# First blocks' loads, masks and three moved steps in an attention, expert and mixing kernel

## The chip, the cores and the metric

The kernel runs on one core of a Trainium2 chip. The metric is the device time of one execution, in microseconds (us). A core has five engines that run side by side, each with its own queue of instructions in a fixed order: TensorE (PE; its weight loads are listed as PEld), VectorE (DVE), ScalarE (ACT), GpSimd (POOL) and SyncE (SP), which here only issues DMAs. ScalarE and GpSimd issue DMAs too. They wait for one another by semaphores.

## The reference

Three parts follow one another. The attention keeps a window of `n_local` = 96 keys and the first `n_global` = 8 keys, adds a bias that falls with the distance, and takes the softmax. The result goes token by token through one of eight experts (a gate decides whether a token takes its own best expert or that of the token before it). A last part mixes over tokens and channels, with a sine and a cosine of a projected angle.

```python
scores = scale * np.matmul(q, k.transpose(0, 1, 3, 2))       # 2 x 8 heads, 768 x 768, head size 64
keep = is_global | is_local
bias = -slopes[:, None, None] * dist[None, :, :]
scores = np.where(keep, scores + bias[None], -1e9)
a = softmax(scores)                                          # rows sum to one
x = a @ v                                                    # -> (2, 768, 512)
...
h = np.maximum(x[b, s] @ w1[e], 0.0)
out[b, s] = p[e] * (h @ w2[e])                               # e: expert of the token
...
theta = x @ w_theta
y = w_tok_r @ (x * cos(theta)) + w_tok_i @ (x * sin(theta))
u = x + y
result = u + np.maximum(u @ w_ch, 0.0)
```

## The kernel before, in words

**Attention.** The 768 tokens of each of two batches are cut into 6 tiles of 128, so there are 12 blocks. `BLOCKS` takes them tile by tile, both batches of a tile in turn; blocks 0 and 1 are the first tiles. A block has four units of two heads. A step `s` is two units, so there are 24 steps, and steps 0 to 3 belong to the first two blocks. In a step TensorE makes the scores of its two units (`qk`, line 558), VectorE adds the bias and takes the extreme of each row (`soft`, line 580), ScalarE takes the exponential (line 590), and TensorE transposes the probabilities of the step before (line 613) and multiplies those of two steps before with the values (line 637). A first tile needs only its own 128 keys; any other needs 256: the 96 before it, 32 of the beginning (for the global keys) and its own 128. The tile `kall` holds 160 key columns for each tile of tokens, and a block reads 256 of them in a row, so the second tile reads the last 96 columns of the first tile's keys.

**Start.** SP issues the window sizes `nn` (line 132), then queries and keys (`load_qk`, lines 466 and 467) and values (`load_v`) of blocks 0, 1 and 2. Block 0's queries and keys come in two halves, so there are four loads for it, in runs of 512 bytes. VectorE casts `nn` (line 508), runs four mask operations (`mask0`, lines 511 to 514) and scales the mask for each head (`biases`, line 525): `biases(0, 0)` and `biases(0, 1)` ahead of the first scores, `biases(0, 2)` and `biases(0, 3)` in step 0. GpSimd makes the constants and then the mask and biases of all other tiles. TensorE starts with `NWARM` = 10 products on zeros (`warm`, line 861) and has one or two of them after the scores of steps 0 to 4 (`WARM`).

**Order by hand.** Every operation of the attention has a short name (`lt10` is the transposed logits of block 10, `pl4` the place of pair 4's tokens in their experts' lists, `px` and `pc` the transpose and copy of the first expert's rows, `lc` the copy of the logits to `lT`, `tk` the token counts). Within the steps they are run by the loop at the end of the attention; what is left after step 23 is listed in `TAIL`. The logits, the token positions and the routing share one bank of TensorE's output memory, the tile `small`.

**Weight jobs.** The weights of the last part (26 pieces, 512 columns each, stored as 64-bit numbers) are converted by `job`: six steps, the absolute value on ScalarE with a shift on VectorE (lines 401 and 402), two integer operations (404, 406), a product (408), a copy on ScalarE with the load of a later piece (411), a difference (414). `job_tick` runs one step. `JATT` lists the attention steps that have one at their end; `TAIL` has three (`jt`); in the expert rounds `tick` adds `JRATE[r]`, divided by 4.5 for rounds 1 to 3 and by 6 otherwise, and runs a step for each whole number reached. `tick` is called from unit 5 on up to unit 55 (a round is eight units), six times per unit, in rounds 1 to 3 not in units 2 and 3, and in rounds 4 to 7 twelve times in every second unit. In the last part `job_upto` (its first call comes with block 1) finishes the job at hand and all that the next product needs.

**Expert rounds.** Rounds 4 to 6 take their weights as they are for the first product (line 1474) and split in two for the second (ScalarE line 1455, VectorE line 1456, TensorE line 1547).

**Last part.** For each block TensorE makes the angle (`th`, line 1783), VectorE and ScalarE reduce it and take sine and cosine (lines 1793 to 1810; line 1797 is the first that reads the product and frees its bank), and TensorE mixes (line 1859).

Of the kernel before, what the change touches and what calls it, by code (L numbers as in the profile page):

```python
# [9 lines left out]
F32 = mybir.dt.float32  # L10
F32R = mybir.dt.float32r
BF16 = mybir.dt.bfloat16
I32 = mybir.dt.int32
AF = mybir.ActivationFunctionType
ALU = mybir.AluOpType
# [35 lines left out]

BLOCKS = [b * NT + t for t in range(NT) for b in range(B)]
TWO_PI = 6.283185307179586
NWARM = 10

WARM = {0: 1, 1: 2, 2: 1, 3: 1, 4: 1}

TAIL = """
ev10 ro4 tk3 tr46 tr47 sc4 cp46 oh4 ho4 cp47 pv44 pv45 yt10 po4 lg10 ri10 lc10 pl4 px pc lt10 ys10 ld10 pv46 pv47 ev11
ri11 mk4 ha0 hb0 hr0 jt yt11 lg11 lc11 jt ha1 hb1 hr1 lt11 ld11 ya0 yb0 sl4 ch5 tk4 ha2 hb2 hr2 ro5 sc5 ys11 ya1 yb1 oh5  # L60
ho5 ha3 hb3 hr3 po5 pl5 ya2 yb2 mk5 rk ha4 hb4 hr4 sl5 tk5 ya3 yb3 ha5 hb5 hr5 en ya4 yb4 ha6 hb6 hr6 ya5 yb5 ha7 hb7
hr7 ya6 yb6 ya7 yb7 ye jt
# [5 lines left out]
CPV0 = (1, 3)  # L68


JATT = (4, 5, 6, 8, 9, 10, 12, 13, 14, 16, 17, 19, 20, 21, 22)
JRATE = (2.0, 1.2, 1.3, 2.9, 2.6, 2.3, 0.4)
T1, T2, T3 = 2, 2, 2
JBUFS = 3
HS = 8
# [25 lines left out]
def kernel(  # L101
# [13 lines left out]
    V, A, G, PE, SP = nc.vector, nc.scalar, nc.gpsimd, nc.tensor, nc.sync  # L115

    const = ctx.enter_context(tc.tile_pool(name="const", bufs=1))
    res = ctx.enter_context(tc.tile_pool(name="res", bufs=1))
# [3 lines left out]
    def ct(shape, dt, name):  # L122
        return const.tile(shape, dt, name=name, tag=name)
# [5 lines left out]


    nn = ct([128, 4], I32, "nn")
    SP.dma_start(nn, n_win.bitcast(I32).partition_broadcast(128))
    wg = ct([128, 4, 32], F32, "wg")


# [216 lines left out]
    wch = [res.tile([128, 4, DM], F32R, tag=f"wch{i}", name=f"wch{i}") for i in range(2)]  # L352
# [93 lines left out]
    with ExitStack() as actx:  # L446
# [4 lines left out]
        pX = actx.enter_context(tc.tile_pool(name="pX", bufs=1, space=PSUM))  # L451
        pM = actx.enter_context(tc.tile_pool(name="pM", bufs=1, space=PSUM))

        qs, vals = {}, {}

        kall = res.tile([128, B, 4, NT * 160], F32, tag="wtokr1", name="kall")

        def load_qk(i):
            n = BLOCKS[i]
            b, t = divmod(n, NT)  # L460
            q = qs[n] = ab.tile([128, 4, 128], F32, tag="q", name="q", bufs=3)
            src = pack[b, t, :, 0:1152].rearrange("p (j c) -> p j c", j=4)
            o = 0 if t else 32

            for j in (slice(0, 2), slice(2, 4)) if n == 0 else (slice(0, 4),):
                SP.dma_start(q[:, j], src[:, j, 0:128])
                SP.dma_start(kall[:, b, j, t * 160 + o : t * 160 + 160], src[:, j, 128 + o : 288])

        def load_v(i):
            n = BLOCKS[i]  # L470
# [8 lines left out]
        wm = ap.tile([128, 512], BF16, tag="wm", name="wm", bufs=1)  # L479
        V.memset(wm, 0.0)  # L480
        G.memset(wg, 0.0)
        for load, i in ((load_qk, 0), (load_qk, 1), (load_v, 0), (load_qk, 2), (load_v, 1), (load_v, 2)):
            load(i)
        for hh in range(2):
            SP.dma_start(
# [4 lines left out]
        wl, wgl = nf[:, 0:1], nf[:, 2:3]  # L490
# [6 lines left out]
        rel = ab.tile([128, 384], F32, tag="rel", name="rel", bufs=1)  # L497
        drop = ab.tile([128, 384], F32, tag="drop", name="drop", bufs=1)
# [9 lines left out]
        V.tensor_copy(nf, nn)  # L508

        def mask0():  # L510
            V.tensor_scalar(rel[:, 0:128], rel[:, 0:128], wl, None, op0=ALU.min)
            V.tensor_scalar(drop[:, 0:128], temp["iota"][:, 0:128], wgl, DROP, op0=ALU.is_ge, op1=ALU.mult)
            V.scalar_tensor_tensor(drop[:, 0:128], rel[:, 0:128], wl, drop[:, 0:128], op0=ALU.is_ge, op1=ALU.mult)
            V.tensor_tensor(drop[:, 0:128], rel[:, 0:128], drop[:, 0:128], op=ALU.add)

        def mask1():
            G.tensor_scalar(drop[:, 128:384], rel[:, 128:384], wl, DROP, op0=ALU.is_ge, op1=ALU.mult)
# [4 lines left out]
        def biases(t, j):  # L522
            bias, c = (bias1, slice(128, 384)) if t else (bias0, slice(0, 128))
            for h in (2 * j, 2 * j + 1):
                (G if t else V).tensor_scalar(bias[:, h], drop[:, c], -8.0 * 2.0 ** -(h + 1), None, op0=ALU.mult)
# [22 lines left out]
        def qk(s):  # L548
            n = units[2 * s][0]
            b, t = divmod(n, NT)  # L550
            W = 256 if t else 128
            for i in range(2):

                sp = [pS.tile([128, 256], F32, tag=f"s{hh}", name=f"s{hh}") for hh in range(2)]
                j = units[2 * s + i][1]
                for hh in range(2):
                    half = slice(64 * hh, 64 * hh + 64)
                    PE.matmul(  # L558
                        sp[hh][:, 0:W],
                        lhsT=qs[n][half, j],  # L560
                        rhs=kall[half, b, j, t * 160 + 160 - W : t * 160 + 160],
                        start=True,
                        stop=True,
                    )
                ust[2 * s + i] = {"s": [x[:, 0:W] for x in sp]}
# [349 lines left out]
        def run(names):  # L915
            for k in names.split():
                ops[k]()
# [5 lines left out]

        warm(NWARM)
        biases(0, 0)
        biases(0, 1)
        mask1()
        for j in range(4):
            biases(1, j)
# [1 line left out]
        for s in range(NS):  # L931
# [4 lines left out]
            qk(s)  # L936
            warm(WARM.get(s, 0))
            run(later.pop((s, 0), ""))
            run(f"sa{u} sb{u}")
            run(later.pop((s, 1), ""))  # L940
            if s:
                run(f"tr{u - 2} tr{u - 1} cp{u - 2}")
# [7 lines left out]
            if s >= 2:  # L950
                run(f"pv{u - 4} pv{u - 3}")
                if s % 2:
                    i, t = s // 2 - 1, (s // 2 - 1) // B
# [20 lines left out]
            if s in (1, 2):  # L974
                job_load()
            if s in JATT:
                job_tick()
# [391 lines left out]
    with ExitStack() as mctx:  # L1369
# [260 lines left out]
        for u in range(64):  # L1630
            r, f = divmod(u, 8)
# [77 lines left out]
            i = f - (1 if r else GP)  # L1709
# [12 lines left out]
            i = f - (2 if r else XF)  # L1722
# [4 lines left out]
    with ExitStack() as hctx:  # L1727
# [260 lines left out]
        for k in range(1, NB):  # L1988
            b, t = divmod(k, NT)
# [110 lines left out]
```

## Time and profile before

| | |
|---|---|
| median of 3 runs | 474.62 us (474.2 to 475.33) |
| profiled execution | 472.67 us, its span 470.9 us |
| mean granted TensorE clock | 0.998 of full speed |
| TensorE busy | 461.1 us (98%), first product at 1.28 us |
| VectorE, ScalarE, GpSimd busy | 349.0, 254.8, 136.3 us |
| attention ends, expert rounds begin | about 114 us |
| expert rounds end, last part begins | about 290 us |

The span runs from the first to the last instruction of one execution; the device time of that execution is a little longer. Times in the rows are microseconds from the span's start. A wait is the idle time of an engine ahead of an instruction, with what ended it. A line of the time line may hold several instructions (x8); its first number is the start, its second the time from the first one's start to the last one's end.

### The profile page before, as it was taken

The numbers are of one execution on the slowest core, as the hardware profiler recorded it, in microseconds if no ns is written. First come the engines' busy times: TensorE is split into PE (matmuls) and PEld (weight loads), VectorE is DVE, ScalarE is ACT, GpSimd is POOL, SyncE is SP. The second block draws the span as 40 slices with busy tenths as digits, with TensorE's granted clock in tenths as the row PEclk, the third lists the DMA queues.
The fourth block names the chain that finished last, engine by engine and source line by source line (L and its number), as shares of the span: only waits on it lengthen the run. The fifth ranks groups of instructions, "written<-read, shape, count | busy, mean of one in ns | idle before, by whom it ended". The sixth has DMA issues, their size and how long they took to land.

```text
span 470.9 us, 9458 instructions
## 1 busy us (share of the span) xinstructions
PE 461.1 (98%) x3311; PEld 382.5 (81%) x3311; DVE 349.0 (74%) x919; ACT 254.8 (54%) x613; POOL 136.3 (29%) x185
## 2 busy tenths in 40 slices
PE   8999999999999999999999999999999999999995
PEld 4677777788888998888777888888888888888885
DVE  5879889868688688888778555578999899751422
ACT  5988787722556675757565454565556355520300
POOL 8602322204041403030513303103543332530400
PEclk9999999999999999999999999999999999999999
DMA  8978678525957788887998972500023000000022
GB/s 239 372 232 271 182 247 271 177 91 183 334 180 243 255 280 273 285 272 268 303 360 295 320 267 66 188 24 22 24 70 130 24 13 11 1 34 35 35 82 89
DMA packets 60410, 82.97 MB, mean 176 GB/s; under 512 B 5528, under 2 KB 39576, under 8 KB 60360
## 3 DMA queue, kind: packets, MB, share of 16 engines
q1 hardware_dynamic: 52500, 62.65, 40.4%
q0 software_dynamic: 4272, 9.92, 6.5%
q10 hardware_dynamic: 3588, 9.77, 5.9%
q8 instruction: 27, 0.44, 0.4%
q14 instruction: 23, 0.19, 0.1%
HBM read 70.94 MB, written 11.38 MB: 175 GB/s over the span
## 4 chain that ended last, share of the span: by engine, by line
PE 84%; DVE 5%; ACT 5%; DMA 2%; issue 1%; POOL 1%; SPq 0%; POOLq 0%; DVEq 0%; ACTq 0%
PE a L1859 18%; PE o L1547 14%; PE h L1491 10%; PE h L1474 8%; PE b L1896 7%; PE th L1783 5%; PE o L1563 3%; PE s L558 3%; PE x L637 3%; ACT pr L590 2%; PE pt L613 2%; PE h L767 2%; PE y L778 2%; PE tr L1323 2%; PE y L654 1%
## 5 line engine op out<-in xcount | busy, mean ns | idle before, releaser
L1859 PE MATMUL a<-wtokr,z 128*128 128x512 f32 x480 | 85.8, 337 | 0.0
L1859 PEld LDWEIGHTS a<-wtokr,z 128*128 128x128 f32 x480 | 73.8, 188 | 9.3
L1547 PE MATMUL o<-w2s,hh 128*128 128x512 f32 x192 | 62.5, 405 | 0.0
L590 ACT ACTIVATE pr<-sm,st 128x256 f32<-128x256 f32 (+1 forms) x96 | 46.0, 482 | 15.2 <-DVE st L580 15.1
L1491 PE MATMUL h<-xT,w1s 128*128 128x288 f32 (+3 forms) x384 | 51.6, 284 | 0.5 <-DVE xT L1329 0.5
L1491 PEld LDWEIGHTS h<-xT,w1s 128*128 128x128 f32 x384 | 48.7, 189 | 3.3 <-issue 0.6
L1456 DVE TENSOR_TENSOR w2s<-raw,w2s 128x512 fp32r<-128x512 f32 x56 | 38.4, 688 | 11.0 <-ACT w2s L1455 10.9
L1474 PEld LDWEIGHTS h<-xT,raw 128*128 128x128 f32 x256 | 37.0, 190 | 4.4 <-issue 3.9
L1474 PE MATMUL h<-xT,raw 128*128 128x192 f32 (+3 forms) x256 | 40.5, 311 | 0.0
L580 DVE CUSTOM_DVE_ANT_0 sm<-s,bias 128x256 f32<-128x256 f32 (+1 forms) x96 | 33.9, 395 | 8.4 <-ACT ps L622 3.8
L1455 ACT ACTIVATE w2s<-raw 128x512 fp32r<-128x512 f32 x56 | 34.9, 625 | 6.0 <-PE h L1474 1.9
L1547 PE MATMUL o<-w2s,hl 128*128 128x512 f32 x96 | 37.8, 394 | 0.0
L1547 PEld LDWEIGHTS o<-w2s,hh 128*128 128x128 f32 x192 | 32.3, 184 | 5.7 <-DVE w2s L1456 0.8
L1599 POOL DMA_DIRECT2D yd<-yo x13 | 8.3, 636 | 77.7 <-ACT yo L1597 77.7
L1904 DVE SCALAR_TENSOR_TENSOR ob<-b,xTf 128x512 f32<-128x512 f32 (+1 forms) x16 | 8.8, 556 | 27.1 <-PE b L1896 27.1
L1815 POOL TENSOR_TENSOR si<-si,yg 128x512 f32<-128x512 f32 x10 | 13.5, 1347 | 51.6 <-ACT si L1808 48.6
L558 PE MATMUL s<-kall,q 64*128 64x256 f32 (+1 forms) x192 | 25.6, 385 | 0.2 <-DMA kall<-in_pack_dram 0.2
L1352 DVE TENSOR_TENSOR w1s<-raw,w1s 128x512 fp32r<-128x512 f32 x32 | 21.8, 686 | 5.2 <-ACT w1s L1351 5.1
L404 DVE SCALAR_TENSOR_TENSOR jw<-jraw,jw 128x512 int32<-128x512 int32 x26 | 24.7, 950 | 0.4
L406 DVE SCALAR_TENSOR_TENSOR jw<-jraw,jw 128x512 int32<-128x512 int32 x26 | 24.6, 945 | 0.1
L613 PE MATMUL pt<-ident,pr 128*128 128x128 f32 x176 | 24.4, 278 | 0.2 <-ACT pr L590 0.2
L637 PE MATMUL x<-ps,vv 128*64 128x128 f32 x352 | 24.5, 279 | 0.0
(290 smaller groups left out, 956.4 us busy)
## 6 DMA issues: line engine op xcount, KB each, us to landing
raw<-in_w_dram SPq DMA_DIRECT2D x60, 512.0 KB, 5.4
vv<-in_pack_dram SPq DMA_DIRECT2D x10, 512.0 KB, 5.2
jraw<-in_w_tokT_dram ACTq DMA_DIRECT2D x10, 512.0 KB, 5.1
w<-in_w_dram SPq DMA_DIRECT2D x16, 256.0 KB, 4.9
kall<-in_pack_dram SPq DMA_DIRECT2D x10, 320.0 KB, 4.8
xd<-xt SPq DMA_DIRECT2D x12, 256.0 KB, 6.1
q<-in_pack_dram SPq DMA_DIRECT2D x11, 256.0 KB, 4.1
jraw<-in_w_tokT_dram ACTq DMA_DIRECT2D x10, 256.0 KB, 5.2
```

The costliest lines, as they stand in the source:

```text
L558: PE.matmul(sp[hh][:, 0:W], lhsT=qs[n][half, j], rhs=kall[half, b, j, t * 160 + 160 - W : t * 160 + 160], start=True, stop=True,)
L580: V.tensor_tensor_reduce(out=sm[:, hh, 0:W], in0=ust[u]["s"][hh], in1=bias[:, 2 * j + hh], scale=-0.125, scalar=BIG, op0=ALU.add, op1=ALU.min,
L590: A.activation(pr[:, hh, 0:W], sm[:, hh, 0:W], AF.Exp, bias=st[:, hh : hh + 1], scale=-1.0, accum_out=sums[n][:, 2 * j + hh : 2 * j + hh + 1],
L613: PE.transpose(pt[:, hh, c], pr[:, hh, c * 128 : (c + 1) * 128], ident)
L637: PE.matmul(xp[64 * hh : 64 * hh + 64, j], lhsT=vv[:, i, h * 64 : (h + 1) * 64], rhs=ps[:, hh, c], start=(c == 0), stop=(c == nch - 1),)
L1455: A.activation(h2, bb[:, o], AF.Copy)
L1456: V.tensor_tensor(l2, bb[:, o], f32(h2), op=ALU.subtract)
L1474: PE.matmul(hp[:, :N], lhsT=pieces[u // 2][1][:, j, o * 128 : (o + 1) * 128], rhs=x[:, j, :N], start=(j == 0), stop=(j == 3),)
L1491: PE.matmul(hp[:, :N], lhsT=wa[:, j], rhs=xa[:, j, :N], start=(k == 0), stop=(k == 11))
L1547: PE.matmul(out[:M], lhsT=ha[:, lo : lo + M], rhs=wa, start=(f == 0 and q == 0), stop=(f == 7 and q == 2),)
L1859: PE.matmul(acc[b][d][o], lhsT=za[:, d * 128 : (d + 1) * 128], rhs=wa[:, lo:hi], start=(t == 0 and n == 0 and (o == 0 or d % 2 == 0)), sto ...
L1896: PE.matmul(op[:, : hi - lo], lhsT=wa[:, d, e * 128 : (e + 1) * 128], rhs=ua[d][:, lo:hi], start=(n == 0), stop=(n == 11),)
```

## The change

- The window sizes `nn` are loaded from ScalarE's queue and no longer from SP's.
- The queries and keys of the first tiles go into a tile of their own, in the room of a weight that is written much later. All 288 columns of each pair of heads come in one piece: two loads of 2304 bytes per row for block 0, one of 4608 bytes for block 1. Their scores read the keys from there. The 96 key columns that the second tiles need are loaded into `kall` by two extra loads, `load_k0`, issued behind the first values and behind the second block's values.
- `mask0` has three operations: the `min` is part of the last one.
- `biases(0, 1)` is run after the scores of the first unit, not ahead of them.
- `NWARM` is 7, and step 0 has two warm-up products.
- `pl4` comes after `lt10` in `TAIL`.
- The job step at the end of attention step 20 is at that of 23.
- `JRATE` is 2.8, 2.8 and 0.7 in rounds 4, 5 and 6 (2.6, 2.3 and 0.4 before).

```diff
-NWARM = 10
-WARM = {0: 1, 1: 2, 2: 1, 3: 1, 4: 1}
+NWARM = 7
+WARM = {0: 2, 1: 2, 2: 1, 3: 1, 4: 1}
...
-ev10 ro4 tk3 ... yt10 po4 lg10 ri10 lc10 pl4 px pc lt10 ys10 ld10 pv46 pv47 ev11
+ev10 ro4 tk3 ... yt10 po4 lg10 ri10 lc10 px pc lt10 pl4 ys10 ld10 pv46 pv47 ev11
...
-JATT = (4, 5, 6, 8, 9, 10, 12, 13, 14, 16, 17, 19, 20, 21, 22)
-JRATE = (2.0, 1.2, 1.3, 2.9, 2.6, 2.3, 0.4)
+JATT = (4, 5, 6, 8, 9, 10, 12, 13, 14, 16, 17, 19, 21, 22, 23)
+JRATE = (2.0, 1.2, 1.3, 2.9, 2.8, 2.8, 0.7)
...
-    SP.dma_start(nn, n_win.bitcast(I32).partition_broadcast(128))
+    A.dma_start(nn, n_win.bitcast(I32).partition_broadcast(128))
...
         def load_qk(i):
+            src = pack[b, t, :, 0:1152]
+            if t == 0:
+                room = res.tile([128, 4, 512], F32, tag=f"wch{b}", name="qk0")
+                qk = room.rearrange("p j c -> p (j c)")[:, 0:1152]
+                for c in (slice(0, 576), slice(576, 1152)) if n == 0 else (slice(0, 1152),):
+                    SP.dma_start(qk[:, c], src[:, c])
+                qk = qk.rearrange("p (j c) -> p j c", j=4)
+                qs[n], k0s[n] = qk[:, :, 0:128], qk[:, :, 160:288]
+                return
             q = qs[n] = ab.tile([128, 4, 128], F32, tag="q", name="q", bufs=3)
-            o = 0 if t else 32
-            for j in (slice(0, 2), slice(2, 4)) if n == 0 else (slice(0, 4),):
-                SP.dma_start(q[:, j], src[:, j, 0:128])
-                SP.dma_start(kall[:, b, j, t * 160 + o : t * 160 + 160], src[:, j, 128 + o : 288])
+            src = src.rearrange("p (j c) -> p j c", j=4)
+            SP.dma_start(q, src[:, :, 0:128])
+            SP.dma_start(kall[:, b, :, t * 160 : t * 160 + 160], src[:, :, 128:288])
+
+        def load_k0(b):
+            src = pack[b, 0, :, 0:1152].rearrange("p (j c) -> p j c", j=4)
+            SP.dma_start(kall[:, b, :, 64:160], src[:, :, 192:288])
...
-        for load, i in ((load_qk, 0), (load_qk, 1), (load_v, 0), (load_qk, 2), (load_v, 1), (load_v, 2)):
+        for load, i in ((load_qk, 0), (load_qk, 1), (load_v, 0), (load_k0, 0), (load_qk, 2), (load_v, 1), (load_k0, 1), (load_v, 2)):
...
         def mask0():
-            V.tensor_scalar(rel[:, 0:128], rel[:, 0:128], wl, None, op0=ALU.min)
             V.tensor_scalar(drop[:, 0:128], temp["iota"][:, 0:128], wgl, DROP, op0=ALU.is_ge, op1=ALU.mult)
             V.scalar_tensor_tensor(drop[:, 0:128], rel[:, 0:128], wl, drop[:, 0:128], op0=ALU.is_ge, op1=ALU.mult)
-            V.tensor_tensor(drop[:, 0:128], rel[:, 0:128], drop[:, 0:128], op=ALU.add)
+            V.scalar_tensor_tensor(drop[:, 0:128], rel[:, 0:128], wl, drop[:, 0:128], op0=ALU.min, op1=ALU.add)
...
-                        rhs=kall[half, b, j, t * 160 + 160 - W : t * 160 + 160],
+                        rhs=kall[half, b, j, t * 160 + 160 - W : t * 160 + 160] if t else k0s[n][half, j],
...
         biases(0, 0)
-        biases(0, 1)
...
             run(f"sa{u} sb{u}")
+            if s == 0:
+                biases(0, 1)
```

## Rows read from the trace of the kernel before

**Rows 1.** the page's part 1: engine, busy us (share of the span), instructions

```profile
PE 461.1 (98%) x3311; PEld 382.5 (81%) x3311; DVE 349.0 (74%) x919; ACT 254.8 (54%) x613; POOL 136.3 (29%) x185
```

**Rows 2.** TensorE's waits, whole span: who <- released by: us, times, longest

```profile
PE th L1783 <- DVE rr L1797: 0.6, 1, 0.6
...
PE small L226 <- ACT lT L223: 0.5, 1, 0.5
...
PE small L226 <- DVE rpt L312: 0.4, 1, 0.4
```

**Rows 3.** VectorE's time line, first 8 us: start, us, line, [idle before]

```profile
3.43 0.23 DVE L508 CAST nf<-nn 128x4 f32<-128x4 int32 x1 [2.20 <-DMA nn<-in_n_win_dram]
3.78 0.29 DVE L511 TENSOR_SCALAR rel<-rel,nf 128x128 f32<-128x128 f32 x1
3.98 0.31 DVE L512 TENSOR_SCALAR drop<-iotas,nf 128x128 f32<-128x128 f32 x1
...
5.10 0.65 DVE L525 TENSOR_SCALAR bias<-drop 128x128 f32<-128x128 f32 x4
5.67 0.28 DVE L580 CUSTOM_DVE_ANT_0 sm<-s,bias 128x128 f32<-128x128 f32 x1
...
7.05 0.28 DVE L580 CUSTOM_DVE_ANT_0 sm<-s,bias 128x128 f32<-128x128 f32 x1
```

**Rows 4.** ScalarE's time line, first and fifth exponential

```profile
5.99 0.40 ACT L590 ACTIVATE pr<-sm,st 128x128 f32<-128x128 f32 x1 [3.88 <-DVE st L580]
...
7.55 0.39 ACT L590 ACTIVATE pr<-sm,st 128x128 f32<-128x128 f32 x1
```

**Rows 5.** ScalarE's time line, around 220 us

```profile
220.07 1.28 ACT L1695 ACT_TABLE_LOAD   x1
```

**Rows 6.** SP's queue, its time line, first 2 us

```profile
0.86 0.39 SPq L132 DMA_DIRECT2D nn<-in_n_win_dram  x1
1.29 0.43 SPq L466 DMA_DIRECT2D q<-in_pack_dram  x1
1.76 0.47 SPq L467 DMA_DIRECT2D kall<-in_pack_dram  x1
```

**Rows 7.** stretch: length, busy of PE, PEld, DVE, ACT, POOL, granted clock, DMA share, GB/s

```profile
1.80:2.70 0.90, 0.90 (x4) 0.34 (x3) 0.00 (x0) 0.31 (x1) 0.83 (x6) 1.00 0.10 19
```

**Rows 8.** time lines, warm-up weight loads (the eighth) and first scores

```profile
4.25 0.15 PEld L861 LDWEIGHTS <-wm 128*128 128x128 bf16 x1 [0.28 <-issue]
...
5.14 0.71 PE L558 MATMUL s<-kall,q 64*128 64x128 f32 x8
```

**Rows 9.** GpSimd's time line: the biases of the second kind of block

```profile
9.69 7.08 POOL L525 TENSOR_SCALAR bias<-drop 128x256 f32<-128x256 f32 x8
```

**Rows 10.** time line, 78.8 to 80.2 us, ScalarE and TensorE

```profile
78.94 0.66 ACT L401 ACTIVATE jm<-jraw 128x512 f32<-128x512 f32 x1
...
79.81 0.33 PE L226 MATMUL small<-ident,lT 128*128 128x128 f32 x1 [0.52 <-ACT lT L223]
```

**Rows 11.** VectorE's time line, after step 23

```profile
90.38 0.16 DVE L260 SCALAR_TENSOR_TENSOR rcb<-rcb,rfe 128x2 bf16<-128x2 bf16 x1
90.92 0.19 DVE L341 TENSOR_TENSOR toks<-toks,small 128x32 f32<-128x32 f32 x1 [0.38 <-PE small L267]
```

**Rows 12.** TensorE's time line, 94.2 to 95.6 us

```profile
95.30 0.30 PE L226 MATMUL small<-ident,lT 128*128 128x128 f32 x1 [0.38 <-DVE rpt L312]
```

**Rows 13.** the stretch of expert round 5, columns as in rows 7

```profile
237.47:258.20 20.73, 20.73 (x129) 16.25 (x129) 16.97 (x38) 11.78 (x24) 5.80 (x9) 1.00 0.93 324
```

**Rows 14.** time lines, 320 to 326 us, VectorE and TensorE

```profile
320.94 0.68 DVE L404 SCALAR_TENSOR_TENSOR jw<-jraw,jw 128x512 int32<-128x512 int32 x1
...
322.38 0.69 DVE L408 SCALAR_TENSOR_TENSOR jw<-jm,jw 128x512 f32<-128x512 f32 x1
...
324.84 0.69 DVE L1797 SCALAR_TENSOR_TENSOR rr<-kk,th 128x512 f32<-128x512 f32 x1
...
325.67 2.10 PE L1783 MATMUL th<-wth,xh 128*128 128x512 f32 x8 [0.62 <-DVE rr L1797]
```

More of the change, by code (lines that the diff above doesn't have):

```diff
@@ L53 @@
 TWO_PI = 6.283185307179586
-NWARM = 10
-WARM = {0: 1, 1: 2, 2: 1, 3: 1, 4: 1}
+NWARM = 7
+WARM = {0: 2, 1: 2, 2: 1, 3: 1, 4: 1}
 TAIL = """
-ev10 ro4 tk3 tr46 tr47 sc4 cp46 oh4 ho4 cp47 pv44 pv45 yt10 po4 lg10 ri10 lc10 pl4 px pc lt10 ys10 ld10 pv46 pv47 ev11
+ev10 ro4 tk3 tr46 tr47 sc4 cp46 oh4 ho4 cp47 pv44 pv45 yt10 po4 lg10 ri10 lc10 px pc lt10 pl4 ys10 ld10 pv46 pv47 ev11
 ri11 mk4 ha0 hb0 hr0 jt yt11 lg11 lc11 jt ha1 hb1 hr1 lt11 ld11 ya0 yb0 sl4 ch5 tk4 ha2 hb2 hr2 ro5 sc5 ys11 ya1 yb1 oh5
@@ L452 @@
         pM = actx.enter_context(tc.tile_pool(name="pM", bufs=1, space=PSUM))
-        qs, vals = {}, {}
+        qs, k0s, vals = {}, {}, {}
         kall = res.tile([128, B, 4, NT * 160], F32, tag="wtokr1", name="kall")
@@ L460, in load_qk @@
             b, t = divmod(n, NT)
-            q = qs[n] = ab.tile([128, 4, 128], F32, tag="q", name="q", bufs=3)
-            src = pack[b, t, :, 0:1152].rearrange("p (j c) -> p j c", j=4)
-            o = 0 if t else 32
-            for j in (slice(0, 2), slice(2, 4)) if n == 0 else (slice(0, 4),):
-                SP.dma_start(q[:, j], src[:, j, 0:128])
-                SP.dma_start(kall[:, b, j, t * 160 + o : t * 160 + 160], src[:, j, 128 + o : 288])
+            src = pack[b, t, :, 0:1152]
[7 more added lines that the diff above has]
+                return
+            q = qs[n] = ab.tile([128, 4, 128], F32, tag="q", name="q", bufs=3)
+            src = src.rearrange("p (j c) -> p j c", j=4)
[4 more added lines that the diff above has]
+            SP.dma_start(kall[:, b, :, 64:160], src[:, :, 192:288])
         def load_v(i):
```

## The prediction

> **What bounds the kernel now.** I read the busy table first, then TensorE's waits over the whole span, then the time lines around each wait. The busy table has TensorE at 461.1 of 470.9 us [rows 1], so time can only come from the 9.8 us in which it idles, or from the start, where the warm-up products count as busy. The list of its waits is short: 0.62 us for VectorE's `rr` in the last phase, 0.52 us for ScalarE's `lT` in one attention step, 0.38 us for VectorE's `rpt` near the end of attention [rows 2]. The change touches the places of all three, which the reader should see before anything else. The start is another matter: there VectorE and ScalarE set the pace and TensorE fills with warm-up products, so the views to read are their time lines.
>
> The profiled execution took 472.67 us, 1.77 more than its span; the median of the three runs is 474.62, 1.95 above it. All terms below are differences on the profiled execution, and I carry them over to the median unchanged.
>
> **The start: masks, loads, warm-up.** VectorE gets the window sizes at 3.43, then runs the mask and the biases, and the first score is reduced at 5.67 [rows 3]; ScalarE's first exponential follows at 5.99 and its fifth at 7.55 [rows 4], 0.39 apart, so by then it is ScalarE that is full. The change takes out the `min` (3.78 to 3.98, so 0.20) and puts the second pair of biases behind the first two scores (four take 0.57 from 5.10 to 5.67, so two are 0.29). The first exponential could start 0.49 earlier. The two biases come back before the third score, however: the fifth score stands behind the same work less the `min`, so it moves from 7.05 to 6.85 and its exponential cannot start before 6.85 + 0.32 = 7.17, where 0.32 is 5.99 less 5.67. That is 0.38 before 7.55, and 0.38 is what the start is worth if the window sizes arrive when they do now.
>
> They need not. Their load goes from SP's queue, where it is ahead of everything, to ScalarE's. There it has nothing ahead: the other table load of this kernel stands right at the line that first needs it [rows 5], so I take the first one to come behind the load; ScalarE's slack before 5.99 covers both. But SP now issues the first block's data at the place of 0.86 instead of 1.29 [rows 6], so the small load shares the engines with a large one. Now it has them alone from 1.8 to 2.7, at a busy share of 0.10 and 19 GB/s (some of it already the next load's) [rows 7]. Bounds: 0.03 earlier, since ScalarE's first work stands at 0.83 against 0.86; 0.9 later, if each of its packets waits for one of the other load, which doubles its 0.9. I take 0.3 late, a third of the way, as it is issued at the same moment and not behind. Net 0.38 - 0.30 = 0.08 gained, between 0.41 gained and 0.52 lost.
>
> The Trainium skill ("DMA: Bandwidth & Descriptors", section "Queues, rings and completion order") says that each DMA engine turns round robin between the queues, a whole packet at a time. Taken literally the small load would wait for about one packet of the large one on each engine; no row of the kernel before shows two queues starting together, and it is the rule that speaks most against this edit. By it the bound of 0.9 would hold, the start would lose 0.52, and the sum below would be 0.86; that is the first rival.
>
> The scores themselves: the eighth warm-up product starts at 4.25 [rows 8], so seven end there. The first loads are issued 0.86 instead of 1.29 and are one piece; the half block of queries and keys was there by 5.14 without a wait when its last load went out at 1.76, so it should be there by 4.24 (0.90 earlier; unknown are only the 32 columns more in each piece). Scores take 0.53 to VectorE, so 4.8, ahead of the biases at 5.18 plus the 0.3. Were they as late as now, they would be ready at 5.67 and the first exponential would gain nothing, the fifth still some. From the engine's first work at 1.28 the seven take 2.97, 0.42 each, which for 512 columns is the 1.2 GHz level; the series is three short, and if the level rose later the first score products would be twice as long, some 0.5 at most, part of it covered by ScalarE. GpSimd's eight biases for the second kind of block are done at 0.85 each from 9.69, the fourth at 13.1 [rows 9]; ScalarE has sixteen exponentials of 0.39 from 5.99 before any of that kind, so it takes the first at 12.2 at the earliest and the fourth some 1.2 later, and half a us gained at the start does not run into them. The two extra loads of 96 key columns and the 32 columns more put about 0.5 MB ahead of later loads; SP issues two loads fewer before the first values and from an earlier start, and no wait for a block's load is among the large ones [rows 2]. I cost it at nothing; without that cover it would be a wait of up to 1.6 (0.5 MB at the 324 GB/s of a filled stretch [rows 13]) less what the earlier issue gives back.
>
> **The step moved from 20 to 23.** Three of the weight job's steps go one step later each (20, 21, 22 to 21, 22, 23). They issue the absolute value on ScalarE and three integer operations on VectorE; none issues a DMA, since the load belongs to the fifth step, which stays in the tail. At the end of step 20 the absolute value runs from 78.94, ahead of `lT`, and TensorE waits 0.52 for it [rows 10]. One step later the next copy of `lT` is two steps off, so nothing waits there; ScalarE is 0.55 later for one step and has idle time after it. At the far end the third operation (0.60 from start to start) lands behind `rcb` (90.38 + 0.08), so VectorE's `toks`, now at 90.92 after a wait of 0.38, starts at 91.06 [rows 11] and the row scan behind it, which TensorE needs at once, is 0.14 late. Net 0.38; bounds 0.52 and 0.
>
> **`pl4` behind `lt10`.** TensorE stands 0.38 at `lt10` (line 226) until VectorE has read the shared bank (line 312) [rows 2, 12]. Placed first, the transpose needs only `lT`, which is there. VectorE's five operations then start some 0.5 later, about 95.2, and with them the store and the marks; the marks' first reader on TensorE comes only after the next block's transposes, so this is covered, and if it were not the price would be up to that 0.5. No DMA but the store of block 10 comes later on SP's queue. Gain 0.38; bounds 0.38 gained, 0.12 lost.
>
> **The rates.** Each job is six steps. Before: 15 in attention and 3 in the tail; then 18 calls at 2.0/6 = 6.0; 36 at 1.2, 1.3 and 2.9 over 4.5 = 9.6, 10.4 and 23.2; 48 at 2.6, 2.3 and 0.4 over 6 = 20.8, 18.4 and 3.2. Sum 18 + 91.6, so 109 steps: 18 jobs and one step. The last phase first finishes the job at hand, so five steps stand in VectorE's way, starting with line 404 at 320.94, and `th` waits 0.62 for line 1797 behind them [rows 14]. After: 22.4, 22.4 and 5.6 in the last three, 18 + 99.6, so 117: 19 jobs and three steps. Lines 404 and 406 are gone from here; line 408 stood at 322.38, so all behind it comes 1.44 earlier. That is more than the 0.62, and TensorE's own work is the next bound. Gain 0.62; bounds 0.62 and 0, if something else of that chain holds `th`.
>
> The eight steps more lie in the expert rounds 4 to 6. A step costs VectorE at most 0.69, and four of round 5's fall where it is busy 16.97 of 20.73 us [rows 13]; 4 x 0.69 makes 19.7. It stays under TensorE, and the split weights are made a pair of units ahead, so I cost it at nothing. One more 512 KB load lies in that stretch, covered the same way.
>
> **Sum.** 0.08 + 0.38 + 0.38 + 0.62 = 1.46. Profiled execution 472.67 to 471.2, median 474.62 to 473.2. Behind 97 us TensorE and the routing chain both start from its products, so the earlier terms carry on.
>
> **Rivals.**
> - *The window sizes or the scores come late.* For it: nothing now runs beside that small load. Against: it is 2 KB and issued first. At 0.9 late the start loses 0.52 and the total is 0.86 gained, 473.8; with the lower clock level as well, 474.3. Chance 0.16.
> - *Another wait takes the place.* The chain to `rcb` runs over VectorE, and TensorE waits there just after the moved steps; and `pl4` later could hold back the tail. Then the two middle terms are gone: 0.08 + 0.62 = 0.70, 473.9. Chance 0.14.
> - *VectorE becomes the bound in rounds 4 and 5.* It decides from the point where a pair of units has more VectorE work than TensorE's 5 us. Six steps per pair are 6 x 0.69 = 4.1 at most; with two weight splits, the activation's remainder and waits for ScalarE that is near 5. Eight steps all on the path would be 8 x 0.69 = 5.5 lost, 478.7; I price half of that, since VectorE's idle time takes the rest: 2.8 - 1.46 = 1.3 slower, 475.9. For it: 82% mean load in round 5 [rows 13]. Against: no TensorE wait in these rounds now. Chance 0.10.
>
> **How the numbers follow.** The forecast has 0.60. Anything within 0.2%, 0.95 us, of 474.62 cannot be told from no change. Of the forecast 0.56 lies below 473.67 and 0.04 above; of the first rival 0.05 and 0.11, of the second 0.04 and 0.10; the third is slower. So faster 0.65, same 0.25, slower 0.10. All upper bounds together gain 0.41 + 0.52 + 0.38 + 0.62 = 1.9, 472.7; the three runs lie 0.4 below and 0.7 above their median, so the range begins at 472.1. Upward it takes in both rivals with the same spread, to 474.8.
>
> **What would show it.** Right: the cast of the window sizes starts before 4.0 and ScalarE's fifth exponential before 7.5; no wait of line 226 for `lT` in step 21, nor for `rpt`; lines 404 and 406 gone from the chain ahead of `th` and its wait with them; TensorE still without waits in rounds 4 to 6. Wrong: the cast at 4.3 or later; a new wait at `rcb` or line 285 larger than 0.5; TensorE waiting for split weights.

## Result: 5.4 us slower, where 1.46 us faster was forecast

The changed kernel takes 479.99 us (median of 5 runs, 479.65 to 481.17), the kernel before in the same rounds 474.62 (474.2 to 475.5). The ratio is 1.0113, 95% interval 1.0094 to 1.0131. The profiled executions lie further apart (481.17 against 472.67, spans 479.4 and 470.9): the one of after is 1.2 above its median, the one of before 1.95 below. So 8.5 us stand between the two traces, and 5.4 are to be explained.

TensorE's share falls only from 98 to 97% [rows 1], which shows little; its waits show more. First the page's busy line of the changed kernel, then its waits (line, releaser, us in total, times, longest).

```profile
PE 465.7 (97%) x3308; PEld 384.1 (80%) x3309; DVE 348.2 (73%) x918; ACT 255.5 (53%) x613; POOL 132.5 (28%) x185
```

```profile
PE s L569 <- DVE st L591: 1.4, 2, 1.2
...
PE few L1575 <- issue: 1.0, 1, 1.0
PE y L665 <- ACT ps L633: 0.9, 3, 0.4
PE s L569 <- DMA qk<-in_pack_dram: 0.8, 1, 0.8
PE o L1559 <- DVE w2s L1468: 0.8, 4, 0.2
PE o L1559 <- DVE hl L1534: 0.6, 1, 0.6
...
PE x L648 <- ACT xT L660: 0.4, 1, 0.4
```

The three waits that the forecast counted on [rows 2] are gone: `th`, and line 226 for `lT` and for `rpt`. New are the first scores (`st`, `qk`), the products with split weights (`w2s`, `hl`), and `xT` in attention.

**The start.** VectorE's and ScalarE's time lines after (start, duration, instruction, idle time before it), to be held against [rows 3, 4]: the window sizes are cast at 5.42 instead of 3.43, the first exponential comes at 7.66 instead of 5.99, the fifth at 10.24 instead of 7.55.

```profile
5.42 0.23 DVE L520 CAST nf<-nn 128x4 f32<-128x4 int32 x1 [4.20 <-DMA nn<-in_n_win_dram]
...
7.33 0.29 DVE L591 CUSTOM_DVE_ANT_0 sm<-s,bias 128x128 f32<-128x128 f32 x1
```

```profile
0.83 0.42 ACTq L132 DMA_DIRECT2D nn<-in_n_win_dram  x1
1.28 1.28 ACT L601 ACT_TABLE_LOAD   x1 [1.28 <-PEq L2065]
7.66 0.40 ACT L601 ACTIVATE pr<-sm,st 128x128 f32<-128x128 f32 x1 [5.10 <-DVE st L591]
...
10.24 0.40 ACT L601 ACTIVATE pr<-sm,st 128x128 f32<-128x128 f32 x1 [0.79 <-DVE st L591]
```

TensorE's time line after: it stands 0.83 ahead of the first scores, and 1.15 behind them, since the score banks come free only when VectorE has read them.

```profile
5.28 0.71 PE L569 MATMUL s<-qk 64*128 64x128 f32 x8 [0.83 <-DMA qk<-in_pack_dram]
5.92 0.61 PE L872 MATMUL small<-wm 128*128 128x512 bf16 x2
7.68 0.70 PE L569 MATMUL s<-qk 64*128 64x128 f32 x4 [1.15 <-DVE st L591]
...
25.85 1.09 PE L648 MATMUL x<-ps,vv 128*64 128x128 f32 x16
```

The stretches of the start after (from:to, then length, busy time of PE, PEld, DVE, ACT and POOL, granted clock, DMA share, GB/s): right behind these holes the granted clock falls to 0.50, the 1.2 GHz level, and stays there for the whole stretch from 9 to 15 us. In the trace of before it is 1.00 in all of these stretches.

```profile
5.00:7.00 2.00, 1.25 (x10) 0.64 (x10) 1.36 (x5) 0.00 (x0) 1.90 (x13) 1.00 0.93 350
7.00:9.00 2.00, 1.10 (x7) 0.91 (x8) 1.98 (x13) 1.30 (x7) 1.82 (x4) 0.89 1.10 349
9.00:15.00 6.00, 6.00 (x33) 3.90 (x32) 3.63 (x22) 4.42 (x21) 5.67 (x8) 0.50 1.10 359
15.00:17.00 2.00, 1.84 (x22) 1.60 (x21) 1.19 (x9) 0.88 (x5) 1.74 (x4) 0.90 1.11 382
```

The `x` product shown last above (25.85) starts at 21.17 before: 4.68 later, and it stays at that to 70 us.

```profile
21.17 1.09 PE L637 MATMUL x<-ps,vv 128*64 128x128 f32 x16
```

**The three moved steps.** The wait of [rows 10] is gone, but in step 22 the absolute value now stands on ScalarE ahead of `xT`, and TensorE waits twice (ScalarE's time line after, then TensorE's):

```profile
88.35 0.67 ACT L401 ACTIVATE jm<-jraw 128x512 f32<-128x512 f32 x1
88.91 0.59 ACT L660 ACTIVATE xT<-x 128x512 f32<-128x512 f32 x1
```

```profile
89.55 1.09 PE L648 MATMUL x<-ps,vv 128*64 128x128 f32 x16 [0.39 <-ACT xT L660]
91.02 0.65 PE L665 MATMUL y<-ident,xT 128*128 128x128 f32 x4 [0.37 <-ACT ps L633]
...
93.03 0.33 PE L226 MATMUL small<-ident,lT 128*128 128x128 f32 x1
```

**The last phase** does what the forecast said: of the begun job only line 408 and what follows it is left ahead of `th`, and `th` has no wait [rows 14]. Line 1809 here is line 1797 before, the one that frees the bank of `th`.

```profile
330.11 0.68 DVE L408 SCALAR_TENSOR_TENSOR jw<-jm,jw 128x512 f32<-128x512 f32 x1
...
332.55 0.69 DVE L1809 SCALAR_TENSOR_TENSOR rr<-kk,th 128x512 f32<-128x512 f32 x1
```

```profile
334.10 2.02 PE L1795 MATMUL th<-wth,xh 128*128 128x512 f32 x8
```

Set side by side by the same product in both traces, TensorE is behind by 4.68 at 21 us, 5.04 at 78 us (see e6), 4.67 at 98 us, 5.45 at 237 us (0.8 lost around the gathers of 110 to 123 us), 7.88 at 262 us (round 5 [rows 13] loses 2.4), 9.2 at 311 us (1.0 of the 1.3 lost is the wait of `few`) and 8.35 at 329 us (the wait of `th` gives 0.85 back). The wait of `few` is 0, 0.3, 0.4 or 0.5 in the traces of the other kernels, whose code is the same there, so I take it for chance and not for a part of the 5.4.

### The profile page after: what moved, and what is told of

Same layout as the page of the kernel before. It is cut to its first block, busy times and chain, and to the rows that moved or that the text cites. A ratio compares the mean times of both kernels' runs of the same rounds, so it can differ in the third digit from the quotient of the medians.

```text
span 479.4 us, 9446 instructions
## 1 busy us (share of the span) xinstructions
PE 465.7 (97%) x3308; PEld 384.1 (80%) x3309; DVE 348.2 (73%) x918; ACT 255.5 (53%) x613; POOL 132.5 (28%) x185
## 4 chain that ended last, share of the span: by engine, by line
PE 79%; DVE 9%; ACT 6%; issue 2%; DMA 2%; POOL 1%; ACTq 0%; POOLq 0%; DVEq 0%
PE a L1871 21%; PE o L1559 12%; PE h L1503 10%; PE b L1908 7%; PE th L1795 6%; PE h L1486 4%; PE s L569 3%; PE x L648 3%; ACT pr L601 2%; PE pt L624 2%; PE y L665 1%; DVE w2s L1468 1%; PE tr L1335 1%; PE o L1575 1%; ACT ps L633 1%
## 5 line engine op out<-in xcount | busy, mean ns | idle before, releaser
L1559 PE MATMUL o<-w2s,hh 128*128 128x512 f32 x192 | 63.5, 408 | 0.8 <-DVE w2s L1468 0.8
L411 ACT ACTIVATE wtokr<-jw 128x512 fp32r<-128x512 f32 x15 | 9.5, 631 | 29.0 <-DVE jw L408 26.1
L404 DVE SCALAR_TENSOR_TENSOR jw<-jraw,jw 128x512 int32<-128x512 int32 x26 | 23.7, 911 | 0.3
L406 DVE SCALAR_TENSOR_TENSOR jw<-jraw,jw 128x512 int32<-128x512 int32 x26 | 23.6, 907 | 0.2
```

Source lines behind the costliest of these rows:

```text
L1559: PE.matmul(out[:M], lhsT=ha[:, lo : lo + M], rhs=wa, start=(f == 0 and q == 0), stop=(f == 7 and q == 2),)
```

## The experiments

Each was timed in five rounds against the kernel before. The medians of before (473.27 to 474.73) come from several chips, so I go by the ratios; 0.1% is 0.47 us. "Behind" is the start of the same TensorE product against the trace of before. It compares one execution with one: at 21 us the traces of kernels with the loads of before lie between 0.02 ahead and 0.83 behind.

**e1, after with the small load first again**

```
-    A.dma_start(nn, ...)
+    SP.dma_start(nn, ...)
```

> The changed kernel with one line put back: the window sizes are loaded by SyncE again, ahead of the first block's data; the one-piece loads, the seven warm-up products, the masks and the moved steps stay. Theory A (the small load, issued beside the large ones, lands 2 us late, and TensorE's clock falls because it stands still meanwhile): the cast of the window sizes starts at 3.4 to 3.9 instead of 5.42, no stretch of the first 25 us shows a granted clock of 0.50, and the time falls by 4 to 5 us, to 475 to 476. Rival B (the one-piece loads or the fewer masks and warm-up products make the start late by themselves): the cast is early, but the scores still come late or the clock still falls, and the time stays above 478. Rival C (the loss sits in the moved steps): the start is repaired and less than 1 us comes back.

475.08; ratio 1.0048 (1.0033 to 1.0062). The cast starts at 3.83, the clock is 1.00 in all stretches to 21 us, and the same `x` product is 0.46 behind. So the place of the small load is worth 1.0113 - 1.0048 = 0.65%, 3.1 us. Both signs of theory A are there, though less came back than the 4 to 5 us expected. 2.3 us are left for something else: in this trace TensorE ends 2.18 behind, with 2.4 lost in round 5 and 0.85 given back at `th`.

```profile
3.83 0.17 DVE L520 CAST nf<-nn 128x4 f32<-128x4 int32 x1 [2.61 <-DMA nn<-in_n_win_dram]
```

**e3, before with the small load alone on ScalarE's queue**

```
-    SP.dma_start(nn, ...)
+    A.dma_start(nn, ...)
```

> The kernel before with one line changed: the window sizes are loaded from ScalarE's queue. Queries and keys still come in pieces of 512 and 640 bytes, and there are ten warm-up products. If any other load beside it makes the small load late, the cast moves from 3.43 to 4.5 or later and the time rises by 1 to 2 us. If it is the one-piece loads that push it back (theirs are packets of 2304 bytes and more), the cast stays below 4.0 and the time within 0.5 us of the kernel before. If the fall of the clock needs only the late mask, it shows a granted clock of 0.50 here too, and the loss is 3 us or more.

473.28; ratio 1.0001 (0.9992 to 1.0011). The cast is 0.32 late, just the 0.3 that I had taken, and it costs nothing that can be measured. What makes the small load late in the changed kernel is what it runs beside.

```profile
3.75 0.17 DVE L508 CAST nf<-nn 128x4 f32<-128x4 int32 x1 [2.53 <-DMA nn<-in_n_win_dram]
```

**e5, after with the first block in four loads of 1152 bytes**

```
-  for c in (slice(0, 576), slice(576, 1152)) if n == 0 else ...
+  for c in [slice(i, i + 288) for i in range(0, 1152, 288)] if n == 0 else ...
```

> The changed kernel, window sizes still on ScalarE's queue, but the first block's queries and keys come in four loads of 1152 bytes per partition instead of two of 2304; the second block's stay one piece. If the small load waits for a packet of the large one between its own (the time by which it is late then goes with the packets' size: 0.3 at 512 and 640 bytes in the kernel before with this load moved, 2.0 at 2304), the cast starts between 3.9 and 4.8 and 1 to 3 us of the changed kernel's loss come back, 477 to 479. If it waits for all of the large loads' bytes, or for something on ScalarE's own queue, the cast stays at 5.4 and the time at 480.

475.07; ratio 1.0036 (1.0023 to 1.0049): 3.7 us back, more than I expected. With pieces of 512 bytes per partition beside it the small load is 0.32 late (e3; only block 2's keys come in 640), with 1152 bytes 0.66, with 2304 bytes 1.99: it grows with the piece, and not with the bytes in all, which are the same in the last two. (Where the load stands first on SP beside the loads of before, ten traces have the cast at 3.43 to 3.46.) A single load is halved along with its piece, however (1024 bytes per partition in e3, 1152 here, 2304 in after), so piece and load are not told apart between these two. The DMA records of the traces have the 128 packets of 16 bytes of the small load from 1.88 to 3.38 us in e3, from 2.18 to 3.60 here and from 2.15 to 4.97 in after, spread among the large ones and not behind them. The rule of the Trainium skill that the prediction weighed ("DMA: Bandwidth & Descriptors", section "Queues, rings and completion order": turns between the queues, a whole packet at a time) agrees with this in kind. The first scores start here at 4.38, near the 4.24 forecast for them. In after they start at 5.28, so the two loads of 2304 bytes beside the small one do not bring the data early.

```profile
4.09 0.17 DVE L520 CAST nf<-nn 128x4 f32<-128x4 int32 x1 [2.87 <-DMA nn<-in_n_win_dram]
```

```profile
4.38 1.23 PE L569 MATMUL s<-qk 64*128 64x128 f32 x8
```

**e2, after with the holes filled by warm-up products**

```
-NWARM = 7;  WARM = {0: 2, ...}
+NWARM = 10; WARM = {0: 7, ...}
```

> The changed kernel with ten warm-up products at the start instead of seven, and seven instead of two behind the first scores; the window sizes stay on ScalarE's queue. The products fill the two holes in which TensorE stood still (0.83 us ahead of the first scores, 1.15 us behind them). If the fall of the clock is a cost of its own beside the late window sizes, the granted clock stays 1.00 through 5 to 17 us, and the 4.7 us of the start shrink to the 1.7 to 2.0 by which the first exponential is late: some 2.5 to 3 us come back, about 477. If the clock falls all the same, or the late mask alone makes the 4.7 us, the time stays at 479.5 to 480.5.

477.05; ratio 1.0083 (1.0070 to 1.0096). The small load is as late as in after (cast at 5.40, first exponential at 7.66), but the granted clock stays at 1.00 and the `x` product starts at 23.86, 2.69 behind instead of 4.68. So 2.0 us of that trace are the clock's, and 2.7 the late mask's; the timing gives the clock 0.3%, 1.4 us, less than the 2.5 to 3 expected.

```profile
9.00:15.00 6.00, 5.55 (x50) 4.04 (x49) 4.61 (x31) 5.05 (x26) 5.67 (x8) 1.00 1.10 358
```

**e6, before with the fewer masks and the moved biases**

```
-            V.tensor_scalar(rel[:, 0:128], rel[:, 0:128], wl, None, op0=ALU.min)
-        biases(0, 1)                          (ahead of the scores)
+            if s == 0: biases(0, 1)           (behind the first two)
```

> The kernel before with the fewer mask operations and the second pair of biases behind the first scores; loads, warm-up and the moved steps are the kernel before's. My prediction gives it 0.38: the first exponential up to 0.49 earlier, the fifth 0.38, so 0.2 to 0.4 us faster. Rival: the two biases now stand between the second and the third score, ScalarE is held up there instead, and GpSimd's masks and the transposes set the pace after the first microseconds: within 0.2 us of the kernel before.

473.89; ratio 1.0018 (1.0004 to 1.0031), rather slower. VectorE is ready at 5.33 (4.88 + 0.45) and stands 0.86 for the scores, whose products start at 5.66: there was nothing for the mask to be early for. In the kernels whose loads are those of before the first scores start between 4.93 and 5.66, from one execution to the next. e3 and, below, e10 and e14 have the same 5.66 with the old masks; their first exponential is at 6.72 to 6.83 and their fifth at 8.28 to 8.38, here they are at 6.52 and 8.29. What the first four win is lost on the two biases behind them. Part of the loss is further on: at 72 us VectorE stands 0.45 ahead of `xt`, and TensorE loses 0.35 by 78 us (the row of before first, then that of e6). All six traces of kernels with the three mask operations have this wait and this loss, e11 too, which keeps the biases ahead of the scores; none of the ten others has. Why one operation less in `mask0` makes VectorE wait there stays open, and so does the rest of the 0.85 that the timing shows.

```profile
4.88 0.45 DVE L524 TENSOR_SCALAR bias<-drop 128x128 f32<-128x128 f32 x2
6.19 0.29 DVE L579 CUSTOM_DVE_ANT_0 sm<-s,bias 128x128 f32<-128x128 f32 x1 [0.86 <-PE s L557]
```

```profile
71.11 0.69 DVE L659 TENSOR_TENSOR xt<-y,sums 128x512 f32<-128x512 f32 x1
```

```profile
72.22 0.69 DVE L658 TENSOR_TENSOR xt<-y,sums 128x512 f32<-128x512 f32 x1 [0.45 <-PE s L557]
```

**e4, before with the three moved steps**

```
-JATT (..., 20, 21, 22); JRATE (..., 2.6, 2.3, 0.4); "lc10 pl4 px pc lt10 ys10"
+JATT (..., 21, 22, 23); JRATE (..., 2.8, 2.8, 0.7); "lc10 px pc lt10 pl4 ys10"
```

> The kernel before with the three moved steps alone (the step of 20 to 23, the five operations behind the transpose of lT, the raised rates); its start is untouched. My prediction gives them 1.38 us together: 473.2. The rival from the changed kernel's trace (TensorE waits for split weights and for the activation's remainder in round 5, some 2.4 us, and the routing chain at line 285 takes back what the step of 20 gained): the time is 0.5 to 1.5 us above the kernel before, with waits of line 1547 in its list.

474.49; ratio 1.0022 (1.0013 to 1.0030): 1.0 slower where I had them 1.38 faster. The next seven runs take them apart.

**e10, the step of 20 to 23 alone** (the first of the three lines above)

> The kernel before with the weight job's three steps one step later each, nothing else. My prediction gives it 0.38 gained. From the trace of the three moved steps together: the wait of 0.5 for lT goes, two waits of 0.4 each come in the next step (ScalarE's absolute value now stands ahead of xT there), and the wait of 0.35 at rcb covers part of it; so between 0.1 gained and 0.3 lost, no difference that can be measured.

474.93; ratio 1.0005 (0.9993 to 1.0017): nothing. TensorE's time line has the two waits of after in its place:

```profile
85.36 1.09 PE L637 MATMUL x<-ps,vv 128*64 128x128 f32 x16 [0.39 <-ACT xT L649]
86.82 0.66 PE L654 MATMUL y<-ident,xT 128*128 128x128 f32 x4 [0.37 <-ACT ps L622]
```

**e14, the five operations behind `lt10` alone** (the last of the three)

> The kernel before with the five operations behind the transpose of lT, nothing else. My prediction gives it 0.38; the traces of two kernels that contain it show TensorE 0.5 to 0.6 earlier behind that place, of which some is lost again at the next gather. So 0.3 to 0.6 faster: just what a timing can tell. If the five operations later hold back the store of block 10 or the marks, no gain.

472.77; ratio 0.9990 (0.9976 to 1.0004). TensorE gains 0.55 at the place, and in this execution loses 0.4 again at the gathers behind it. A gain of 0.4 agrees with it, and so does none.

**e7, the raised rates alone** (the middle one)

> The kernel before with the raised rates alone. From the traces of the changed kernel and of the three moved steps: round 5 loses 2.3 us (TensorE late by split weights and the activation's remainder), the wait of 0.6 to 0.85 in the last phase goes, so 1.3 to 1.6 us slower. If those waits come from the three steps together (the jobs would stand otherwise without the step of 20), less than 0.8 is lost.

475.02; ratio 1.0032 (1.0020 to 1.0044): 1.5 slower, 2.4 lost in round 5 and 0.85 gained at `th`. ScalarE, VectorE and TensorE at one place of round 5:

```profile
248.15 0.63 ACT L411 ACTIVATE wtokr<-jw 128x512 fp32r<-128x512 f32 x1 [2.90 <-DVE jw L408]
...
249.68 0.64 ACT L1455 ACTIVATE w2s<-raw 128x512 fp32r<-128x512 f32 x1
```

```profile
247.43 0.69 DVE L408 SCALAR_TENSOR_TENSOR jw<-jm,jw 128x512 f32<-128x512 f32 x1
...
250.35 0.69 DVE L1456 TENSOR_TENSOR w2s<-raw,w2s 128x512 fp32r<-128x512 f32 x1 [2.01 <-ACT w2s L1455]
```

```profile
252.19 0.50 PE L1547 MATMUL o<-w2s,hl 128*128 128x512 f32 x1 [0.55 <-DVE hl L1522]
```

The reader is to see that VectorE is late here although it stood idle for 2.01. ScalarE's copy (line 411) comes in its order ahead of the weight split, and waits 2.90 for VectorE's four steps of the job; then VectorE waits for the split. In the trace of before the copy stood behind two splits (246.16 and 246.95, copy at 249.26).

**e12, the raised rates, with the copies of round 5 on VectorE**

```
-        A.activation(wh, wf, AF.Copy)
+        (V.tensor_copy(wh, wf) if 15 <= k <= 17 else A.activation(wh, wf, AF.Copy))
```

> The kernel before with the raised rates alone, and in the three jobs of round 5 the copy of line 411 made by VectorE instead of ScalarE: more work for VectorE (three copies of 0.4 to 0.7 us), and no step of the job in which ScalarE stands waiting for VectorE with the activation and the weight splits queued behind it. If round 5 loses 2.3 us because VectorE has too much to do, the loss grows to 3 or more, 476 to 477. If it loses them because ScalarE waits in its order for the job (2.9 us ahead of line 411) and VectorE then waits for ScalarE's split (2.0 us), the loss shrinks to less than 1 us, and with the shorter chain ahead of th the time is 0.6 below to 0.4 above the kernel before.

474.57; ratio 1.0028 (1.0014 to 1.0042); round 5 loses 2.0. Neither expectation is met, and the edit missed its aim: the job's load is issued on ScalarE's queue and waits for the same steps, so ScalarE still stands 3.15 (the row of its time line). Inconclusive.

```profile
255.03 0.38 ACT L1520 ACTIVATE hh<-h 128x256 fp32r<-128x256 f32 x1 [3.15 <-DVE jw L408]
```

**e13, the same steps, with two calls between the fourth and the copy**

```
-JRATE (..., 2.8, 2.8, 0.7)
+JRATE (..., 2.8, 3.55, 0.7)
+        if 15 <= k <= 17: yield; yield
         A.activation(wh, wf, AF.Copy)
```

> The kernel before with the raised rates, and in the three jobs of round 5 two empty calls between the fourth VectorE step and ScalarE's copy (with the load behind it); round 5's rate is 3.55 instead of 2.8 to make up for the empty calls, so that VectorE does the same 117 steps. If the loss is ScalarE's wait in its order, ScalarE no longer stands 2 to 3 us ahead of line 411, round 5 loses less than 1.2 instead of 2.3, and the time is within 0.5 us of the kernel before. If it is VectorE's amount of work, or that its steps lie too close together, round 5 still loses 2 us or more, and the time is 1.2 to 2 us above.

473.73; ratio 1.0016 (1.0005 to 1.0028). Round 5 loses 0.9 instead of 2.4 with the same work on VectorE. At the place shown for e7 ScalarE waits 1.21 instead of 2.90, and VectorE no longer waits there; but its two earlier waits for a split in this round (2.2 and 1.2) stay, and ScalarE still waits 2.50 and 2.02 at the next two copies. So in the traces 1.5 of the 2.4 lost go with the order on ScalarE at that place. For the 0.9 that are left VectorE's load is not excluded. The time is above what I expected (0.16%, 0.8 us); by the timing half of e7's loss is gone, with intervals that overlap.

```profile
248.55 0.63 ACT L411 ACTIVATE wtokr<-jw 128x512 fp32r<-128x512 f32 x1 [1.21 <-DVE jw L407]
```

**e8, fewer steps instead of more, and the five operations moved**

```
-JRATE (..., 2.6, 2.3, 0.4)
+JRATE (..., 2.6, 2.3, 0.25)
```

> The kernel before with the five operations moved behind the transpose of lT, and the last rate lowered from 0.4 to 0.25: 108 steps of the weight job instead of 109, which makes 18 whole jobs and leaves none begun. If the wait in the last phase comes from the job that is begun there, it goes without any load in round 5, and the transposition gains its 0.38: 0.8 to 1.2 us faster. If the chain ahead of th is bound by something else, only 0.2 to 0.4 comes back; and if the 109th step was worth something, less.

477.23; ratio 1.0081 (1.0067 to 1.0094), against my expectation. With 108 steps `th` does not wait and TensorE is 0.85 earlier there, but the next job is begun too late for its reader, and TensorE waits 3.0 for it (its waits, then the stretch behind this one, columns as in rows 7). Behind the wait the granted clock falls to 0.50 from 360 to 366 us; it is 1.00 there in the trace of before. TensorE goes from 1.27 ahead to 4.80 behind, so the 109th step was worth 6.1 us in this trace: 3.0 by the wait and 3.1 behind it.

```profile
PE a L1859 <- ACT wtokr L411: 3.0, 1, 3.0
```

```profile
360.00:366.00 6.00, 5.54 (x16) 4.55 (x17) 1.73 (x3) 0.41 (x1) 0.00 (x0) 0.50 0.40 134
```

**e9, four steps more in round 6 alone, and the five operations moved**

```
-JRATE (..., 2.6, 2.3, 0.4)
+JRATE (..., 2.6, 2.3, 0.85)
```

> The kernel before with the five operations behind the transpose of lT, and the last rate raised from 0.4 to 0.85: 113 steps, 18 whole jobs and five of six steps of the next, all four steps more in round 6. With 108 steps the chain ahead of th was 0.85 shorter but the next job began too late (a wait of 3.0 for wtokr). Here the job is begun as in the kernel before and only its last step is left. If both readings hold, round 5 loses nothing, th doesn't wait, nothing waits 3 us for wtokr, and the transposition gives its 0.3 to 0.6: 0.9 to 1.4 us faster. If round 6 is as full of VectorE work as round 5, TensorE waits there, and the gain is below 0.5.

474.16 against 474.73; ratio 0.9985 (0.9977 to 0.9994): 0.7 faster. Rounds 5 and 6 lose nothing (the product of 272.10 in the trace of before starts at 272.04), and `th` does not wait. The gain rests on the timing: this trace loses 0.6 at the gather of `rows` and 0.6 around `few` behind 288 us, and ends 0.43 behind.

```profile
272.04 2.23 PE L1474 MATMUL h<-xT,raw 128*128 128x144 f32 x16
```

**e11, e9 with a mended start**

```
 after's one-piece loads, the first block in four of 1152 bytes, nn on SyncE
 NWARM = 8; three mask operations; biases(0, 1) ahead of the scores
 JATT of before; JRATE (..., 2.6, 2.3, 0.85); pl4 behind lt10
```

> The one-piece loads without what made them late: window sizes on SyncE ahead of them, the first block in four loads of 1152 bytes per partition, eight warm-up products, three mask operations but the second pair of biases in front of the scores as in the kernel before; the step of 20 unmoved, the five operations moved, 113 steps of the job. If the scores' data come earlier in fewer, larger packets, and the small load ahead of them isn't held up, the cast stands at 3.4 to 3.8, the first exponential at 5.6 to 5.9, and the start gives 0.2 to 0.5 more than the kernel before with the last two edits alone (that is 1.2 to 1.8 faster than the kernel before). If the one-piece loads cost later what they give at first (the loads of 96 key columns, more bytes ahead of the values), it is no faster than that kernel.

473.99; ratio 0.9982 (0.9973 to 0.9990): 0.85 faster than before, not to be told from e9. The first exponential comes at 5.85, as expected, but in the trace TensorE is 0.17 behind at 30 us. A start that is 0.14 earlier is not kept.

## Why the prediction was wrong

- **The step that failed first: the small load "0.3 late", with 0.9 as its bound.** It is 1.99 late. The bound came from a doubling of the 0.9 that the load took alone [rows 7]; it had no term for the size of the pieces or loads beside it, which the change raises from 512 to 2304 bytes per piece. The 0.3 was right for pieces of 512 bytes (e3). The scores' data, forecast for 4.24, came at 5.28 beside it. The first rival named this mechanism; its price (0.52 lost) was a sixth of the 3.1 to 3.7 us that e1 and e5 get back.
- **The cold clock "some 0.5 at most".** In the trace it costs 2.0 (e2, 1.4 by the timing). I looked at the warm-up products that were left out at the start, and not at what TensorE does when the mask is late: with three warm-up products fewer it stands twice between 4.45 and 7.68. With the mask early the same seven products keep the clock (e1). The risk that was priced, a level that rises late, did not come: the first scores take 0.71 in both traces. (The prediction read the 1.2 GHz level off the first products, 0.42 each, where [rows 7] print 1.00; two later ones take 0.61 together. So that column does not show the first microseconds.)
- **The masks, "0.38 is what the start is worth".** Nothing at the start, and 0.35 lost at 72 us (e6). [Rows 3, 8] have the scores ready just when the mask is, in one execution; the data land up to 0.5 later in others.
- **The step of 20 to 23, 0.38.** Nothing (e10). I said that "nothing waits there" one step later. I had looked for `lT` alone; the next copy on ScalarE is `xT`, and TensorE waits 0.39 and 0.37. The 0.35 that `rcb` gives back [rows 11] covers part of it.
- **`pl4` behind `lt10`, 0.38.** The wait is gone, as forecast; timed alone, 0.5 with an interval that reaches to zero.
- **The rates, 0.62.** The gain at `th` is there, and larger (0.85). The "eight steps more" at nothing cost 2.4 us in round 5. The third rival had a price for this (2.8) and the place, but not the mechanism: I added up VectorE's work (19.7 of 20.73 us), which fits, and did not ask in which order ScalarE meets the job's copy and the weight splits. That order made up 1.5 of the 2.4 in the traces (e13).
- **The sum.** By the ratios: small load and clock 3.1 to 3.7, moved steps 1.0, masks 0.85 (0.2 to 1.5): 5.0 to 5.6, against 5.4; that the parts add up is taken, since they were measured in different kernels. The range's lower end did not follow from its own sum (472.7 less 0.4 is 472.3, not 472.1), which changes nothing here. Two of the signs that the prediction named against itself were seen: the cast later than 4.3, and TensorE waiting for split weights.

## What to carry to other kernels

A small load that the first work waits for goes ahead of the large ones on the same queue; beside them on another queue its delay grew with the size of their pieces, or of the single loads. When an edit can make TensorE stand still near the start, price the fall of its clock too, and look at what would fill the hole; the same holds for a hole in the middle (e8). Before work is added to an engine that has room, follow the in-order neighbour that takes its result: a copy that waits holds up all that stands behind it, and it may come back as a wait of the engine with the room.

## What the runs showed of the hardware

- A load of 2 KB on a second queue was 0.32, 0.66 and 1.99 us late beside pieces of 512 (e3), 1152 (e5) and 2304 bytes per partition (after). First on the same queue it was 0.40 late ahead of pieces of 2304 bytes (e1) and 0.03 ahead of 1152 (e11).
- Behind two holes of 0.83 and 1.15 us the granted clock was 0.50 from 9 to 15 us, with TensorE busy throughout (after); with the holes filled it was 1.00 (e2). Behind one hole of 2.98 us it was 0.50 from 360 to 366 us, with TensorE busy for 5.54 of the 6.00 (e8).
- A stall shorter than the list of waits shows hides in a group's busy time. In e7's round 5 the listed waits add up to 1.1 of the 2.4 lost. A pair of `hh` products that takes 0.63 in the trace of before takes 1.05 in that of e4 (the same pair, first before, then e4):

```profile
256.32 0.63 PE L1547 MATMUL o<-w2s,hh 128*128 128x512 f32 x2
```

```profile
258.01 1.05 PE L1547 MATMUL o<-w2s,hh 128*128 128x512 f32 x2
```
